# Two of four blocks of x inside the first nine steps of the attention loop, and wo in sixteen reads

## The chip, the cores and the metric

The kernel runs on one core of a Trainium2 chip. The metric is the device time of one execution in microseconds. The core has five engines that work side by side, each in the order of its own instructions: PE (matrix products), DVE (vector work), ACT (activation functions), POOL (a second, slower vector engine) and SP (which only issues transfers). Transfers run on sixteen DMA engines; nearly all of them are issued by SP and run in one queue.

## The reference

A block of a transformer with adaptive layer norm, 2048 tokens of 640 features. Cut to what matters here:

```python
mod = silu(c) @ w_mod                       # six rows of 640: sa, ca, ga, sb, cb, gb
h = layernorm(x) * (1 + ca) + sa
q = (h @ wq)                                # 32 heads of 128
p = softmax(q @ k_cache.T * 128 ** -0.5)    # 2048 keys for each head
x = x + ga * ((p @ v_cache) @ wo)           # 4096 -> 640
h = layernorm(x) * (1 + cb) + sb
x = x + gb * B(h)                           # layer norm, w1, gelu, shifts, w2, layer norm, w3, gelu, w4
```

All inputs are bf16. K and V are caches of 32 heads x 2048 keys x 128.

## The kernel before, in words

**The front.** x is read in four blocks of 512 tokens (`load_x`), each block as four tiles of 128 tokens. For a block, `stats` makes mean and variance on DVE (`bn_stats`, `bn_aggr`) and the root on ACT; `normed` takes the reciprocal and normalises on DVE. `to_hT` transposes the block on PE, in five slices of 128 features, four 128x128 transposes each, into a bank of PSUM, and copies the slice out to `hT` with scale and shift, even slices on ACT and odd ones on DVE. Scale and shift come from the first part of w_mod (`load_mod(0, ...)`) by `cols`, 50 narrow products. `q_head0` makes the queries of head 0 for a block from `hT`: five products of 512 columns and a copy on ACT. The front does this for blocks 0, 1, 2 and for the transposes of block 3. The remaining four rows of modulation (`mod_rows`, five chunks of five products and an ACT copy) and the queries of block 3 stand in steps 0 to 2.

While the front runs, its data lies in the ring of 20 slots that the loop uses later for probabilities: x in slots 1 to 5, the first part of w_mod in 6 to 9, the second part and small constants from 13 on. wo has its own memory (40 KB a partition) and is read by one transfer of 5 MB at the end of the front's list of reads.

**The loop.** One step `s` handles 128 queries of one head against all 2048 keys; a head has 16 steps, 32 heads make 512. `qk` makes the scores in two halves on PE. DVE takes each half to `negS` with its running minimum (L598, two of 1.15 us a step). POOL joins the two minima (L603). ACT makes the exponential of the 2048 keys into slot `s % 10` of the ring (L606). The probabilities must then be transposed: for two or three steps of a head PE does it (`PE_STEPS`), for the others SP issues a DMA transpose, mostly for two steps at a time (L233). Nine steps later (`PVD = 9`) `pv` multiplies the transposed probabilities with V (L313, 16 products), ACT copies the result out every second step (L585), POOL divides by the sum and writes to memory. The queries of the next head (`q_piece`, `q_evac`) fill PE's gaps. In steps 2, 6 and 10 of a head SP also issues the reads of K (transposing), wq and V of later heads; V comes in rows of one key, 256 bytes each.

All of this is an order written out by hand: the program text appends each operation to its engine's list, and waits follow from named keys that an operation reads and writes. So what stands first in the text stands first in the engine's queue, and an operation that waits holds up all behind it on its engine. In the first nine steps there is no `pv` yet.

After the loop come the product with wo and the second half of the block, which the change does not touch.

The places that matter: `load_x`, `load_mod`, `load_wq`, `load_k`, `load_v` (reads), `stats`, `normed`, `to_hT`, `q_head0`, `mod_rows` (front), and in the loop

```python
if not is_pe(s):
    if s % 2 == 1 and not is_pe(s - 1):
        transpose(s - 1, 2)
    elif s % 2 == 1 or is_pe(s + 1):
        transpose(s, 1)
```

Of the kernel before, what the change touches and what calls it, by code (L numbers as in the profile page):

```python
# [9 lines left out]
F32 = mybir.dt.float32  # L10
# [113 lines left out]
def bass_adaLN_cond__mha_block_cached__mixer_s_mlp__prompt_kernel(  # L124
# [21 lines left out]
    with ExitStack() as es:  # L146
# [9 lines left out]
        if True:  # L156
            with ExitStack() as es1:
# [35 lines left out]
                wmod = flat[:, WO_:WO_ + KT * 2 * D].rearrange("p (k n) -> p k n", k=KT)  # L193
                RO = 13 * SK
                wmodr = flat[:, RO:RO + KT * 4 * D].rearrange("p (k n) -> p k n", k=KT)
                BO = RO + KT * 4 * D
                s_bc = flat[:, BO:BO + KT * 128].rearrange("p (k q) -> p k q", k=KT)
                ones_f = flat[:, BO + KT * 128:BO + KT * 128 + 256].bitcast(F32)
                SO = BO + KT * 128 + 256
                st = flat[:, SO:SO + NQT * 24].bitcast(F32).rearrange("p (t z) -> p t z", t=NQT)  # L200
                CO = SO + NQT * 24
                c_f = flat[:, CO:CO + 2 * KT].bitcast(F32)
                mcol = flat[:, CO + 2 * KT:CO + 6 * KT].bitcast(F32)
                c_sb = flat[:, CO + 6 * KT:CO + 7 * KT]
                s_col = flat[:, CO + 7 * KT:CO + 8 * KT]
                IO = CO + 8 * KT
                ident = flat[:, IO:IO + 128]
                assert IO + 128 <= 2 * RP * SK and XO + NQT * D <= WO_ and WO_ + KT * 2 * D <= 10 * SK
# [111 lines left out]
                WMK = ringk(WO_, WO_ + KT * 2 * D)  # L320
                WRK = ringk(RO, 2 * RP * SK)
                XK = [ringk(XO + cc * 4 * D, XO + (cc + 1) * 4 * D) for cc in range(NQC)]

                def load_x(cc):
                    G.dma("sync", lambda e: e.dma_start(
                        x_sb[:, 4 * cc:4 * cc + 4], x2d[cc * 512:(cc + 1) * 512, :].rearrange("(t p) d -> p t d", p=128)),
                        ("x", cc), w=[("x", cc)])

                def load_mod(part, dst, n0, n1):
                    G.dma("sync", lambda e: e.dma_start(  # L330
                        dst, w_mod[:, n0:n1].rearrange("(k p) n -> p k n", p=128)), ("wm", part), w=[("wm", part)])

                def load_c(e):
                    with nc.allow_non_contiguous_dma(reason="tiny c vector"):
                        return e.dma_start(c_sb, c[0].rearrange("(kt p) -> p kt", p=128))
# [15 lines left out]
                G.op("gpsimd", lambda g: g.memset(ident, 0.0), w=["id0"])  # L351
                G.op("gpsimd", lambda g: g.memset(ones_f, 1.0), w=["onesf"])
                G.op("gpsimd", lambda g: g.affine_select(out=ident, in_=ident, pattern=[[-1, 128]],
                                                         compare_op=ALU.not_equal, fill=1.0, base=0, channel_multiplier=1),
                     r=["id0"], w=["ident"])
                G.op("gpsimd", lambda g: g.tensor_copy(identf[:], ident), r=["ident"] + ringk(IO, IO + 128), w=["identf"])
                G.op("gpsimd", lambda g: g.memset(Vaug[:, :, :, 128:130], 1.0), w=["ones"])
                G.op("scalar", lambda a: a.activation(s_col, c_sb, ACT.Silu), r=["c"], w=["scol"])
                G.op("scalar", lambda a: a.activation(c_f, c_sb, ACT.Silu), r=["c"], w=["cf"])
                for k in range(KT):  # L360
                    G.op("gpsimd", lambda g, k=k: g.tensor_scalar(out=s_bc[:, k, :], in0=ones_f, scalar1=c_f[:, k:k + 1],
                                                                  scalar2=1.0, op0=ALU.mult, op1=ALU.mult),
                         r=["onesf", "cf"] + WRK, w=[("sbc", k)])

# [11 lines left out]
                def stats(cc):  # L376
                    for t in range(4 * cc, 4 * cc + 4):
                        for z in range(2):
                            G.op("vector", lambda v, t=t, z=z: v.bn_stats(st[:, t, 6 * z:6 * z + 6], x_sb[:, t, z * HD:(z + 1) * HD]),  # L379
                                 r=[("x", cc)], w=[("st", t, z)])  # L380
                    for t in range(4 * cc, 4 * cc + 4):
                        G.op("vector", lambda v, t=t: v.bn_aggr(mv[:, t, :], st[:, t, :]),
                             r=[("st", t, 0), ("st", t, 1)] + WRK, w=[("mv", t)])
                    G.op("scalar", lambda a: a.activation(sd[:, 4 * cc:4 * cc + 4], mv[:, 4 * cc:4 * cc + 4, 1], ACT.Sqrt, bias=float(EPS)),
                         r=[("mv", t) for t in range(4 * cc, 4 * cc + 4)], w=[("sd", cc)])

                def normed(cc):
                    G.op("vector", lambda v: v.reciprocal(rstd[:, 4 * cc:4 * cc + 4], sd[:, 4 * cc:4 * cc + 4]),
                         r=[("sd", cc)], w=[("rstd", cc)])
                    for t in range(4 * cc, 4 * cc + 4):  # L390
                        G.op("vector", lambda v, t=t: v.tensor_scalar(
                            out=x_sb[:, t], in0=x_sb[:, t], scalar1=mv[:, t, 0:1], scalar2=rstd[:, t:t + 1],
                            op0=ALU.subtract, op1=ALU.mult),
                            r=[("rstd", cc), ("mv", t)], w=[("xh", t)])

                def to_hT(cc):
                    for k in range(KT):
                        b = (4, 5, 3, 4, 5)[k % 5] if cc == NQC - 1 else (cc * KT + k) % 6

                        def f(t, k=k, b=b):  # L400
                            for z in range(4):
                                ins = t.transpose(TB[b][:, z * 128:(z + 1) * 128], x_sb[:, 4 * cc + z, k * 128:(k + 1) * 128], ident)
                            return ins
                        G.op("tensor", f, r=["ident"] + [("xh", 4 * cc + z) for z in range(4)] + XK[cc] + ringk(IO, IO + 128), w=[TK[b]])
                        if k % 2 == 0:
# [3 lines left out]
                                r=[TK[b], "mcol"] + WRK, w=[("hT", cc, k)])  # L409
                        else:  # L410
# [3 lines left out]
                                r=[TK[b], "mcol"] + WRK, w=[("hT", cc, k)])  # L414
# [6 lines left out]
                stats(0)  # L421
                normed(0)
                stats(1)
                G.op("tensor", cols, r=["scol", ("wm", 0)] + WMK, w=[("J", 1)])
                G.op("scalar", lambda a: a.copy(mcol[:, 0:KT], JB[1][:, 0:KT]), r=[("J", 1)], w=["mcol0"])
                G.op("scalar", lambda a: a.add(mcol[:, KT:2 * KT], JB[1][:, KT:2 * KT], 1.0), r=[("J", 1), "mcol0"], w=["mcol"])
                normed(1)
                to_hT(0)
                for cc in range(NQC):
                    if cc + 2 < NQC:  # L430
                        stats(cc + 2)
                        normed(cc + 2)
                    if cc + 1 < NQC:
                        q_head0(cc)
                        to_hT(cc + 1)

                mone = small[:, 0:4]
                G.op("gpsimd", lambda g: g.memset(mone, -1.0), w=["mone"] + [("mv", t) for t in range(NQT)])
                bank(("q", 0, NQC - 1))
                MROW = [(n0, min(n0 + 512, 4 * D)) for n0 in range(0, 4 * D, 512)]  # L440

                def mod_rows(i):
                    n0, n1 = MROW[i]
                    bank = PO[:, (i % 2) * 512:(i % 2) * 512 + n1 - n0]
# [5 lines left out]
                    G.op("tensor", f, r=[("sbc", k) for k in range(KT)] + [("wm", 1)] + WRK, w=[("O", i % 2)])  # L450
                    G.op("scalar", lambda a: a.copy(mod_bc[:, n0:n1], bank), r=[("O", i % 2)], w=[("mod", i)])
# [39 lines left out]
                wof = wo[:].rearrange("p h n -> p (h n)")  # L491
# [60 lines left out]
                for s in range(NG + PVD + LAG):  # L552
# [3 lines left out]
                    if s <= 2:  # L556
                        for i in ((0,), (1, 2), range(3, len(MROW)))[s]:
                            mod_rows(i)
                    if s == 3:
                        G.op("gpsimd", lambda g: g.tensor_scalar(  # L560
                            out=mod_bc[:, 2 * D:3 * D], in0=mod_bc[:, 2 * D:3 * D], scalar1=1.0, scalar2=1.0, op0=ALU.add, op1=ALU.mult),
                            r=[("mod", i) for i in range(len(MROW))], w=["mod"])
# [346 lines left out]
```

## Time and profile before

| | us |
|---|---|
| median of three runs (lowest, highest) | 1546.83 (1545.79, 1552.67) |
| the profiled execution | 1551.33 |
| its span, first to last instruction | 1549.2 |
| PE, DVE, ACT, POOL busy | 1467.1, 1374.3, 1256.5, 622.3 |
| PE waiting for a landed transpose, in all | 27.0 |
| the read of wo: issued at, landed after | 30.83, 16.7 |
| first minimum of step 0 (DVE) starts | 35.23 |
| first exponential (ACT) starts | 38.84 |

The profile is of one execution of its own, 4.5 us above the median of the three others. Busy time counts work on the engine; instructions that wait, branch or issue a transfer are not in it, and SP's rows are issues. "idle before <- X" says what ended an idle time. PEld is the loading of weights into PE, which overlaps PE. A wait is put down to the releaser that came last by the profile, which need not be the true one.

### The profile page before, as it was taken

To read this page: it belongs to the slowest core of one execution; us is meant where nothing else is said; L and a number is where in the kernel's file an instruction comes from. 1 tells how busy PE (TensorE), PEld (TensorE's weight loads), DVE (VectorE), ACT (ScalarE), POOL (GpSimd) and SP (SyncE) were. 2 spreads that over 40 slices of the span, in tenths; PEclk is the share of its full clock that TensorE was granted. 3 is DMA by queue.
4 is the path that set the end of the run, shared out by engine and by line. 5 is a ranking of instruction groups with operands and counts; after the bars stand their busy time and mean duration, and the time that the engine had idled before them with its cause. 6 is when DMAs were issued, how large, how long until landed. Compare 5 with 4: busy or idle time off the path is not lost.

```text
span 1549.2 us, 32502 instructions
## 1 busy us (share of the span) xinstructions
PE 1467.1 (95%) x13446; PEld 911.4 (59%) x12663; DVE 1374.3 (89%) x2431; ACT 1256.5 (81%) x1177; POOL 622.3 (40%) x1397
## 2 busy tenths in 40 slices
PE   4899999999999999999999999999999899999999
PEld 2466666666656566666666665666565665554545
DVE  6999999999999999999999999999999737667425
ACT  4999999999999999999999999999999800034230
POOL 0144444444444444444444444444444433323100
PEclk9999999999999999999999999999999999999999
DMA  9999999999999999999999999999999999825100
GB/s 301 243 216 248 246 239 239 238 228 241 239 241 225 241 239 247 229 244 239 233 239 244 236 235 239 238 239 242 227 237 223 243 241 195 155 58 131 35 22 35
DMA packets 1156183, 330.32 MB, mean 213 GB/s; under 512 B 1136640, under 2 KB 1150016, under 8 KB 1156032
## 3 DMA queue, kind: packets, MB, share of 16 engines
q1 hardware_dynamic: 1147552, 307.10, 101.1%
q0 software_dynamic: 6144, 16.79, 3.6%
q10 hardware_dynamic: 2336, 4.34, 0.8%
q8 instruction: 104, 1.70, 0.5%
q14 instruction: 47, 0.39, 0.1%
HBM read 43.48 MB, written 19.40 MB: 41 GB/s over the span
## 4 chain that ended last, share of the span: by engine, by line
ACT 58%; PE 20%; DVE 10%; DMA 7%; issue 3%; POOL 2%; POOLq 0%; DVEq 0%
ACT ring L606 47%; PE Sps L540 9%; DVE negS L598 8%; DMA ring<-ring 6%; ACT ring L272 4%; PE Sps L846 4%; ACT Of L585 3%; ACT kv L255 3%; PE QPp L797 2%; PE Oaug L797 2%; PE PTp L313 1%; PE Sps L782 1%; DVE ring L379 1%; POOL o_scratch L469 1%; DMA kv<-Of 0%
## 5 line engine op out<-in xcount | busy, mean ns | idle before, releaser
L598 DVE TENSOR_SCALAR_CACHE_REDUCE negS<-Sps 128x1024 f32<-128x1024 f32 x1024 | 1174.8, 1224 | 21.2 <-PE Sps L15 20.5
L606 ACT ACTIVATE ring<-negS,small 128x2048 bf16<-128x2048 f32 x512 | 1068.9, 2190 | 10.9 <-POOL small L603 10.2
L313 PEld LDWEIGHTS PTp<-kv,ring 128*128 128x128 bf16 x8192 | 556.2, 98 | 337.8 <-issue 94.7
L313 PE MATMUL PTp<-kv,ring 128*128 128x129 bf16 x8192 | 646.8, 221 | 28.2 <-DMA ring<-ring 27.0
L15 PE MATMUL Sps<-kv 128*128 128x512 bf16 x1009 | 382.6, 379 | 11.3 <-DVE negS L598 7.2
L603 POOL TENSOR_SCALAR small<-small 128x1 f32<-128x1 f32 x512 | 145.8, 285 | 601.1 <-DVE negS L598 601.1
L299 PE MATMUL Sps<-kv 128*128 128x512 bf16 x955 | 367.6, 385 | 14.7 <-DVE negS L598 5.2
L462 POOL TENSOR_SCALAR On<-Of,small 128x128 bf16<-128x128 f32 x512 | 189.9, 371 | 13.0
L299 PEld LDWEIGHTS Sps<-kv 128*128 128x128 bf16 x1024 | 98.2, 96 | 120.3 <-DVE negS L598 87.5
L585 ACT COPY Of<-PTp 128x259 f32<-128x259 f32 x256 | 139.6, 545 | 17.1 <-PE PTp L313 17.1
L455 POOL TENSOR_TENSOR small<-Of,small 128x4 f32<-128x4 f32 x128 | 133.1, 1040 | 11.5 <-ACT Of L585 11.5
L469 POOL DMA_DIRECT2D o_scratch<-On x128 | 103.4, 808 | 40.8 <-POOL On L462 37.2
L248 PE MATMUL Oaug<-hTx,kv 128*128 128x512 bf16 x258 | 97.8, 384 | 5.1 <-DVE hTx L411 4.8
L248 PE MATMUL QPp<-hTx,kv 128*128 128x512 bf16 x259 | 96.7, 378 | 3.0 <-ACT hTx L406 2.3
L727 ACT ACT_TABLE_LOAD x1 | 1.3, 1283 | 111.8 <-POOL hTx L745 111.8
L598 DVE DVE_READ_ACCUMULATOR negS<-Sps 128x1 f32 x1024 | 89.2, 87 | 0.0
L640 POOL TENSOR_SCALAR negS<-negS 128x1 f32<-128x1 f32 x48 | 24.4, 509 | 124.1 <-DVE negS L649 124.1
L540 PE MATMUL Sps<-wo,negS 128*128 128x128 bf16 (+1 forms) x503 | 69.9, 298 | 0.5
L540 PE MATMUL Sps<-wo,hTx 128*128 128x512 bf16 (+1 forms) x502 | 69.3, 298 | 0.5
L850 DVE TENSOR_TENSOR ring<-Sps,ring 128x640 f32<-128x640 f32 x15 | 12.4, 824 | 59.5 <-PE Sps L846 59.5
L654 DVE TENSOR_TENSOR ring<-Sps,mod_bc 128x640 f32<-128x640 f32 x16 | 13.1, 821 | 57.8 <-PE Sps L540 57.8
L265 PE MATMUL QPp<-identf,ring 128*128 128x128 f32 x320 | 61.8, 275 | 0.1
(88 smaller groups left out, 1068.6 us busy)
## 6 DMA issues: line engine op xcount, KB each, us to landing
kv<-in_A_v_cache_dram SPq DMA_DIRECT2D x32, 512.0 KB, 4.9
o_scratch<-On POOLq DMA_DIRECT2D x128, 128.0 KB, 4.9
kv<-in_A_wq_dram SPq DMA_DIRECT2D x32, 160.0 KB, 3.2
wo<-in_A_wo_dram SPq DMA_DIRECT2D x1, 5120.0 KB, 16.7
ring<-ring SPq DMA_TRANSPOSE x240, 7.1
ring<-in_A_x_dram SPq DMA_DIRECT2D x5, 640.0 KB, 6.6
ring<-in_w_mod_dram SPq DMA_DIRECT2D x1, 3200.0 KB, 13.5
out_dram<-wo SPq DMA_DIRECT2D x15, 160.0 KB, 1.8
```

What stands on the lines that cost most here:

```text
L15: return t.add_instruction(mybir.InstMatmult(name=t.bass.get_next_instruction_name(), ins=[t.lower_ap(rhs), t.lower_ap(lhsT)], outs=[t.low ...
L248: G.op("tensor", lambda t: t.matmul(JB[jb], wq[:, hb, q, :], hT[:, q, cc * 512:(cc + 1) * 512], start=(q == 0), stop=(q == KT - 1)), r=[(" ...
L299: ins = (t.matmul if c2 == 0 else partial(same_weights, t))(Sps[:, col:col + 512], QT[:, hb, j * 128:(j + 1) * 128], KTs[:, hb, col:col + ...
L313: ins = t.matmul(ob[:, 0:129], pt, Vaug[:, hb, kt, 0:129], start=(kt == 0), stop=(kt == NKT - 1))
L455: G.op("gpsimd", lambda g: g.tensor_tensor(out=rl[:, 4 * b:4 * b + 4], in0=Of[:].rearrange("p a z d -> p (a z) d")[:, 4 * b:4 * b + 4, 128 ...
L462: G.op("gpsimd", lambda g: g.tensor_scalar(out=On[:, b, z, :], in0=Of[:, 2 * b + z // 2, z % 2, 0:128], scalar1=rl[:, 4 * b + z:4 * b + z ...
L469: G.dma("gpsimd", lambda e: e.dma_start(o_scr[jj // 2:jj // 2 + 2, :, hh].rearrange("a p z d -> p a (z d)"), On[:, b].rearrange("p (a z) d ...
L540: ins = t.matmul(YB[b][:, c0:c0 + cw], OTj[pr % 2][:, 2 * hh + z, :], wo[:, hh, c0:c0 + cw], start=(hh == 0), stop=(hh == H - 1))
L585: G.op("scalar", lambda a, p=p: a.copy(Of[:, p % 4].rearrange("p z d -> p (z d)")[:, 0:259], PO[:, (p % 2) * 512:(p % 2) * 512 + 259]), r= ...
L598: G.op("vector", lambda v, half=half, dst=dst, src=src, r8=r8: v.tensor_scalar(out=dst, in0=src, scalar1=-SCALE, scalar2=None, op0=ALU.mul ...
L603: G.op("gpsimd", lambda g, r8=r8: g.tensor_scalar(out=nm[:, r8:r8 + 1], in0=nm0[:, r8:r8 + 1], scalar1=nm1[:, r8:r8 + 1], scalar2=None, op ...
L606: G.op("scalar", lambda a, s=s, r8=r8: a.activation(Pb[:, s % RP, :], negS[:, s % 3, :], ACT.Exp, bias=nm[:, r8:r8 + 1], scale=-1.0), r=[( ...
```

## The change

Where the staging lies: x block 0 and 1 now lie in ring slots 4 to 6, block 2 and 3 in slots 7 to 9, the first part of w_mod in slots 0 to 3; the second part of w_mod and all small constants lie in wo's memory, which is why wo cannot be read as long as they are used.

Reads: c as a row of five partitions, issued by ACT and turned into a column by a small product on PE; SP's order is x0, first part of w_mod, x1, wq of heads 0 and 1, K of head 0, x2, x3, second part of w_mod, V of head 0, K of head 1. wo is read in sixteen parts of two heads (320 KB each), one in step 11 of every odd head, in the last head in step 4.

Work: `stats` can do part of a block, and takes the root on POOL (add, then power -0.5), not on ACT; ACT loads the table of the exponential once in the front. The front does block 0 in full, block 1 to its normalising and half of the statistics of block 2. `first_steps(s)`, called at the end of step s, does the rest: block 1's transposes in step 0, block 1's queries and block 2's normalising in step 1, the slices of block 2 in steps 2 to 4, statistics of block 3 in 3 and 4, block 2's queries and block 3's normalising in 5, slices of block 3 in 6 to 8, its queries in 9, and the rows of modulation in steps 4, 5, 8 and 9.

`to_hT` now issues all transposes of a call and then all copies. In step 0 its five slices share two banks, so each copy finds there what was transposed last: slices 0 and 2 of block 1 receive slice 4, and slice 1 receives slice 3. The last slice of block 3 is transposed after the exponential of step 8 has been written over two of the four tiles it reads, and the queries of head 0 for block 3 are made with the weights that step 6 has loaded for head 2 in the same buffer. The amount of work is that of the reference; these values are others.

```diff
-                XO = SK
-                x_sb = flat[:, XO:XO + NQT * D].rearrange("p (t d) -> p t d", t=NQT)
-                WO_ = 6 * SK
+                wmod = flat[:, 0:KT * 2 * D].rearrange("p (k n) -> p k n", k=KT)
+                XO = [4 * SK, 4 * SK + 4 * D, 7 * SK, 7 * SK + 4 * D]
+                x_of = lambda cc: flat[:, XO[cc]:XO[cc] + 4 * D].rearrange("p (t d) -> p t d", t=4)
+                wmodr = wof[:, 0:KT * 4 * D].rearrange("p (k n) -> p k n", k=KT)
...
+                WOP = H // 16
+                def load_wo(i):
+                    G.dma("sync", lambda e: e.dma_start(
+                        wo[:, i * WOP:(i + 1) * WOP], A_wo[i * WOP * 128:(i + 1) * WOP * 128, :].rearrange("(h p) n -> p h n", p=128)),
+                        ("wo", i % 2), w=["WOR"] + (["wo", "woz", "wo4"] if i == 15 else []))
+                G.dma("scalar", lambda e: e.dma_start(c_row, c[0].rearrange("(kt p) -> kt p", p=128)), "c", r=WOR, w=["c"])
                 load_x(0)
-                G.dma("sync", load_c, "c", w=["c"])
+                load_mod(0, wmod, 0, 2 * D)
                 load_x(1)
-                load_mod(0, wmod, 0, 2 * D)
+                load_wq(0)
+                if H > 1:
+                    load_wq(1)
+                load_k(0)
                 for cc in range(2, NQC):
                     load_x(cc)
-                load_wq(0)
-                load_k(0)
+                load_mod(1, wmodr, 2 * D, 6 * D)
                 load_v(0)
-                load_mod(1, wmodr, 2 * D, 6 * D)
                 if H > 1:
-                    load_wq(1)
                     load_k(1)
-                G.dma("sync", lambda e: e.dma_start(wo[:], A_wo.rearrange("(h p) n -> p h n", p=128)), "wo", w=["wo", "woz", "wo4"])
...
-                    G.op("scalar", lambda a: a.activation(sd[:, 4 * cc:4 * cc + 4], mv[:, 4 * cc:4 * cc + 4, 1], ACT.Sqrt, bias=float(EPS)),
+                    G.op("gpsimd", lambda g: g.tensor_scalar(out=sd[:, 4 * cc:4 * cc + 4], in0=mv[:, 4 * cc:4 * cc + 4, 1], scalar1=float(EPS),
+                                                             scalar2=1.0, op0=ALU.add, op1=ALU.mult),
...
+                    G.op("gpsimd", lambda g: g.tensor_tensor(out=rstd[:, 4 * cc:4 * cc + 4], in0=sd[:, 4 * cc:4 * cc + 4], in1=mh4, op=ALU.pow),
...
-                stats(0)
+                stats(0, 0, 4)
                 normed(0)
-                stats(1)
+                stats(1, 0, 2)
...
+                to_hT(0, range(KT), range(KT), (1, 3))
+                stats(1, 2, 4)
+                q_head0(0)
...
+                stats(2, 0, 2)
                 normed(1)
-                to_hT(0)
-                for cc in range(NQC):
...
+                def first_steps(s):
+                    if s == 0:
+                        to_hT(1, range(KT), (4, 5, 4, 5, 4))
+                        stats(2, 2, 4)
+                    if s == 1:
+                        q_head0(1)
+                        normed(2)
+                    if s in (2, 3, 4):
+                        k = 2 * (s - 2)
+                        to_hT(2, range(k, min(k + 2, KT)), (4, 5), (1, 3))
+                    if s == 3:
+                        stats(3, 0, 2)
+                    if s == 4:
+                        stats(3, 2, 4)
+                        mod_rows(0, 1)
+                    if s == 5:
+                        q_head0(2)
+                        normed(3)
+                        mod_rows(1, 0)
+                        mod_rows(2, 1)
+                    if s in (6, 7, 8):
+                        k = 2 * (s - 6)
+                        to_hT(3, range(k, min(k + 2, KT)), (4, 5), (1, 3))
+                    if s == 8:
+                        mod_rows(3, 1)
+                    if s == 9:
+                        q_head0(3)
+                        mod_rows(4, 1)
...
+                        if j == (4 if h + 1 == H else 11) and h % 2 == 1:
+                            load_wo(h // 2)
+                        first_steps(s)
```

More of the change, by code (lines that the diff above doesn't have):

```diff
@@ L330, in load_mod @@
                     G.dma("sync", lambda e: e.dma_start(
[L331 to L335, printed above, removed]
+                        dst, w_mod[:, n0:n1].rearrange("(k p) n -> p k n", p=128)), ("wm", part), r=WOR, w=[("wm", part)])
@@ L357, in bass_adaLN_cond__mha_block_cached__mixer_s_mlp__prompt_kernel @@
                 G.op("gpsimd", lambda g: g.memset(Vaug[:, :, :, 128:130], 1.0), w=["ones"])
[L358 to L363, printed above, removed]
+                G.op("tensor", lambda t: t.matmul(JB[0][:, 0:KT], c_row, ident[0:KT, 0:KT], start=True, stop=True),
+                     r=["c", "ident"] + WOR, w=[("J", 0)])
@@ L393, in normed, with to_hT @@
                             op0=ALU.subtract, op1=ALU.mult),
[L394 to L398, printed above, removed]
+                            r=[("rstd", cc), ("mv", u)], w=[("xh", u)])
+                def to_hT(cc, ks, banks, onv=()):
+                    xs = x_of(cc)
+                    for k, b in zip(ks, banks):
@@ L405, in to_hT @@
-                        if k % 2 == 0:
+                        G.op("tensor", f, r=["ident"] + [("xh", 4 * cc + z) for z in range(4)] + XK[cc] + WOR, w=[TK[b]])
+                    for k, b in zip(ks, banks):
+                        if k not in onv:
                             G.op("scalar", lambda a, k=k, b=b: a.activation(
@@ L449, in f @@
                         return ins
[L450 to L451 removed]
+                    G.op("tensor", f, r=[("sbc", k) for k in range(KT)] + [("wm", 1)] + WOR, w=[("O", b)])
+                    G.op("scalar", lambda a: a.copy(mod_bc[:, n0:n1], bank), r=[("O", b)], w=[("mod", i)])
+                def first_steps(s):
[26 more added lines that the diff above has]
+                        mod_rows(4, 1)
+                    if s == 10:
+                        G.op("gpsimd", lambda g: g.tensor_scalar(
+                            out=mod_bc[:, 2 * D:3 * D], in0=mod_bc[:, 2 * D:3 * D], scalar1=1.0, scalar2=1.0, op0=ALU.add, op1=ALU.mult),
+                            r=[("mod", i) for i in range(len(MROW))], w=["mod"])
+                        G.op("gpsimd", lambda g: g.memset(mone, -1.0), w=["mone"] + [("mv", t) for t in range(NQT)])
                 def rcp(gr):
```

117 lines of the change are left out of this document (57 added, 60 removed).

## The prediction

> **What bounds the kernel now.** I read the page's busy shares first, then the stages of the loop, then SP's queue row by row, then who waits for a landed transpose, and last the first 65 us.
>
> ```profile
> PE 1467.1 (95%) x13446; PEld 911.4 (59%) x12663; DVE 1374.3 (89%) x2431; ACT 1256.5 (81%) x1177; POOL 622.3 (40%) x1397
> ...
> 60.00:200.00 140.00, 136.95 (x1354) 89.25 (x1253) 140.00 (x247) 139.58 (x126) 62.59 (x145) 1.00 1.18 237
> ...
> 1000.00:1200.00 200.00, 189.11 (x1868) 121.60 (x1730) 194.93 (x341) 196.70 (x176) 93.10 (x214) 1.00 1.21 232
> ```
>
> In the second and third line the columns are stage, its length, then busy time of PE, PEld, DVE, ACT and POOL, the clock, the DMA share and GB/s. Early in the loop DVE and ACT are full. Late in it nothing that computes is full: something else sets the pace. It is SP's queue (start, length, what):
>
> ```profile
> 742.10 4.61 SPq L233 DMA_TRANSPOSE ring<-ring  x1
> ...
> 746.75 14.66 SPq L233 DMA_TRANSPOSE ring<-ring  x3
> ...
> 761.46 2.05 SPq L216 DMA_TRANSPOSE kv<-in_A_k_cache_dram  x1
> 763.55 4.50 SPq L233 DMA_TRANSPOSE ring<-ring  x1
> ...
> 768.10 0.58 SPq L220 DMA_DIRECT2D kv<-in_A_wq_dram  x1
> 768.73 5.13 SPq L233 DMA_TRANSPOSE ring<-ring  x1
> ...
> 773.91 4.56 SPq L233 DMA_TRANSPOSE ring<-ring  x1
> 778.51 0.58 SPq L225 DMA_DIRECT2D kv<-in_A_v_cache_dram  x1
> ```
>
> Each row starts within 0.05 us of the end of the one before: 742.10 + 4.61 = 746.71, next 746.75, and so on. From 98 us to the end of the loop it has no larger gap than 0.45 us. So SP (the issue, and the transfers that hold it back) works all the time, and falls behind ACT: the pair of transposes of a head's first two steps is issued 1.6 us after its exponential in head 2 (120.66, 122.25), 5.1 in head 10 (415.27, 420.37), and it stays near that (3.8 in head 30), because PE then waits for it. PE's waits for landed transposes, first of 200 to 400 us, then of 1000 to 1240 (total, times, longest):
>
> ```profile
> PE PTp L313 <- DMA ring<-ring: 1.2, 2, 0.8
> ...
> PE PTp L313 <- DMA ring<-ring: 10.2, 10, 2.3
> ```
>
> From exponential to exponential a head takes (341.62 - 120.66)/6 = 36.83 us between heads 2 and 8, ACT's pace, and (1161.97 - 415.27)/20 = 37.34 us between heads 10 and 30, SP's. The front:
>
> ```profile
> 4.84 3.24 DVE L379 BATCH_NORM_STATS2 ring<-ring 128x6 f32<-128x320 bf16 x8 [4.84 <-DMA ring<-in_A_x_dram]
> ...
> 22.78 1.06 PE L248 MATMUL QPp<-hTx,kv 128*128 128x512 bf16 x4 [0.67 <-DVE hTx L411]
> ...
> 29.16 1.89 PE L248 MATMUL Oaug<-hTx,kv 128*128 128x512 bf16 x4 [4.20 <-DVE hTx L411]
> ...
> 35.23 1.23 DVE L598 TENSOR_SCALAR_CACHE_REDUCE negS<-Sps 128x1024 f32<-128x1024 f32 x1 [1.85 <-PE Sps L15]
> ...
> 63.01 2.00 ACT L606 ACTIVATE ring<-negS,small 128x2048 bf16<-128x2048 f32 x1 [0.29 <-POOL small L603]
> ```
>
> Step 0's minimum starts at 35.23; step 9's exponential at 63.01, and ACT hardly idles from there to 200.
>
> **Part 1, the sixteen reads of wo.** The one read lies in the front today: issued at 30.83, landed 16.7 us later, behind K of head 1, which landed at 32.8. It holds up one transpose (issued 44.58, landed 51.23), nine steps before its reader, so taking it out gains nothing on the path. Fifteen of the sixteen parts now stand on SP's full queue; the last falls into head 31, which reads no K, V or wq, and I cost it at nothing. A part is a sixteenth of the old read: 14.7 us alone on the queue (32.8 to 47.5) / 16 = 0.92 us. Bounds: the rows of wq (160 KB, 0.58 us issue, and about 0.5 us longer next transposes) scaled by rows of memory, 256 against 640, give 0.4; V (512 KB: 0.58 us, and the single transpose behind it takes 4.6 instead of 2.1) scaled by bytes, 320/512 of 3.1, gives 1.9. I take 0.92, the same tensor in the same rows. As SP is never idle, a part moves all that is queued behind it: 15 x 0.92 = +13.8 us (6 to 28). At first that is lag, which SP may build up to about 5 us; but it does so in the kernel before too, only by head 10 instead of 5, so the end moves by the full sum. Queued behind a part are the pairs of steps 12 to 15; behind those, PE's second product, then the scores, DVE, ACT.
>
> The Trainium skill (DMA: Bandwidth & Descriptors, Anatomy of one DMA) gives a transfer a fixed 2.0 us beside its bytes; by that a part is 2.75 us and the sum 41. The rows above speak against it: SP goes on 0.05 us after the issue of V, so such a latency lies in the landing, not in the queue.
>
> **Part 2, the front.** I walk each engine's new order with durations from rows: half a minimum 1.145 (2.29 a step), exponential 1.905, from the minimum's end to the exponential 0.51, ACT copy 0.475, ACT transpose copy 0.69, DVE's 0.455, statistics of a block 3.15 and 0.41, normalising 1.43, a 512-column matmul 0.215 and 0.64 from the first scores to DVE.
>
> x0 lands as before at 4.84. Now w_mod's first part comes next (1.6 MB at the 400 GB/s of these slices: 9.0 instead of 12.35), so the columns of shift and scale leave PE at 10.5 instead of 14.0. The inverse root moves from ACT and DVE to POOL: 0.29 + 1.04 (the 128x4 power, L455) against 0.45, so normalising block 0 starts at 9.83 (before 8.90), its transposes at 11.4, the last ACT copy ends at 14.5, the queries of block 0 at 15.8. DVE goes on with blocks 1 and 2a (x2 lands near 16) and block 1's normalising to 19.3. K of head 0 lands near 14. So step 0 starts at 19.3, 15.9 us earlier. The table loads of 1.28 us at 7.10 and 37.55 go.
>
> The small edits cost nothing on the path: c as a row, its product on PE, the constants and the early table load lie before 9.0, while the engines wait for w_mod; the copies of c (5 x 0.35 on POOL) lie behind block 1's root, where POOL waits for step 0; the rows of w_mod are read only after the loop, and their landing (30.3 before, much the same now) is ahead of step 4.
>
> Then what is moved comes back. DVE does inside the steps 3.68 + 1.43 + 0.91 of statistics, normalising and copies for block 3, and for block 2 the same less 1.83: 10.2 us. With no stall step 10 would start at 19.3 + 10 x 2.29 + 10.2 = 52.4; before it did at 62.49. That is the most this part can gain, 10.1 us. But DVE stalls:
>
> - step 2, 1.3: ACT copies five slices of block 1 after step 0's exponential (24.0 to 27.4), PE's queue waits for them with block 1's queries before step 2's scores.
> - steps 3 and 4, 1.4: PE makes the next two slices after the scores and DVE stands for its copy of the second, behind ACT's copy of the bank.
> - step 6, 1.5: eleven matmuls of rows of w_mod, five of block 2's queries, and PE waiting for ACT's copies of both banks, before and inside the scores.
> - steps 7 and 8, 1.5: as 3 and 4.
> - step 9, 4.65: the last slice of block 3 lies in ring slots 8 and 9, so its transposes, queued behind step 8's scores and written after step 8's exponential (56.3 to 58.2), wait for that exponential. Behind them on PE: five matmuls of w_mod and step 9's scores. DVE, done at 55.8, gets them at 60.45.
> - step 10, 2.2: block 3's queries and the last five rows, 2.15 us more on PE in step 9.
>
> Sum 12.55, so step 10 starts at 64.95. Step 9's exponential comes at 63.25 (before 63.01), that of step 11 at 70.04 (before 67.55): +2.5 us, and ACT is full from there as before. SP has caught up with ACT at that point in both kernels (gaps of 1.3, 0.3 and 2.6 us between 74 and 98), so its full stretch starts 2.5 us later too. Bounds: -10.1 with no stall, and +7 if PE runs at half pace in each of about eight stalls, 0.6 us more each.
>
> That pace is in the rows above: four matmuls took 1.06 us at 22.78 after an idle of 0.67, and 1.89 at 29.16 after 4.20 of idle. In my walk PE idles 2.8 us in step 8; the seven matmuls behind it, to the first scores, would at half pace add 1.5 us. The Trainium skill (TensorE: Matmul & The Clock Gate, the HAM clock gate) puts the fall to half rate at about 3.4 us without work, and the two rows agree; by it the 2.8 us stay just below, and the sum stays.
>
> **Sum.** +2.5 + 13.8 = +16.3 us. The profiled execution takes 1551.33 (span 1549.2 and 2.1 around it), which would become 1567.6; the median of the runs is 4.5 lower, 1546.83, so I predict 1563.1.
>
> **Rivals.**
> - A, the parts are hidden: their bytes run while SP still writes the next transposes' descriptors. For it: an unhindered pair takes 4.1 to 4.2 us of SP (60.78, 65.04), so SP may be bound by issuing. Against: the single transpose behind V took 4.6. Then a part costs its issue at most; with 0.2 left of it, 3.0 + 2.5: about 1552.
> - B, faster: DVE's order in steps 0 to 9 does not stall as walked, above all in step 9, and the parts are hidden. Front -10 and parts 0: 1537. It decides where the stalls stay below 7 us and the parts below 0.2 us. Against: the wait for step 8's exponential is in the order of the instructions.
> - C, a part costs as V by bytes, 1.9 us, or PE runs the front at half pace: 15 x 1.9 + 2.5 = +31, 1578. By the fixed latency above, 43 and 1590.
> - D, the reads of x2 and w_mod land later than I think, step 0 starts no earlier than 25 us: 6 us on all steps, 1569.
>
> **How the numbers follow.** My forecast 0.58, A 0.18, B 0.10, C 0.08, D 0.06. The time is that of the first. Its own range is 1554 to 1572 (parts 0.63 to 1.3 us, front -3 to +5). The 8-in-10 range reaches into A and C: 1547 to 1574. About 0.5%, 7.7 us, is what can be told from no change. Faster needs B nearly whole: 0.10. Same takes A, the weak end of B and the cheap end of the forecast: 0.20. Slower 0.70.
>
> **What would show it.** The first minimum near 19 us; a DVE idle of over 4 us before step 9's, released by PE; exponentials of step 9 and 11 near 63 and 70. SP gapless from about 100 us, with fifteen rows of wo in it, PE's wait for landed transposes well over the 27.0 us of before and starting before 360 us, and heads 10 to 30 at 37.8 us each. I am wrong if SP shows gaps in the loop, if heads keep 37.3, or if step 11's exponential starts before 62 us.

## The result and the profile after

The changed kernel takes 1566.03 us (median of 6 runs, 1561.42 to 1569.05) against 1548.3 of the kernel before (6 runs): ratio 1.0111, 95% interval 1.0089 to 1.0133. It is slower by 17.7 us; forecast were 16.3. The profiled execution took 1569.05 us, its span is 1567.2, 18.0 longer than before. (The median of 1546.83 given above for the kernel before was that of the first three of the six runs.)

The page of the changed kernel: busy shares, and the two largest groups of DVE and ACT (busy, mean of one, idle before them and its releaser).

```profile
PE 1472.7 (94%) x13448; PEld 903.9 (58%) x12664; DVE 1375.4 (88%) x2425; ACT 1259.5 (80%) x1175; POOL 630.0 (40%) x1406
...
L635 DVE TENSOR_SCALAR_CACHE_REDUCE negS<-Sps 128x1024 f32<-128x1024 f32 x1024 | 1177.3, 1222 | 36.5 <-PE Sps L15 35.5
L643 ACT ACTIVATE ring<-negS,small 128x2048 bf16<-128x2048 f32 x512 | 1037.1, 2062 | 34.3 <-POOL small L640 33.4
```

No engine's work grows by nearly that much: PE is busy 5.6 us longer, POOL 7.7, ACT 3.0, DVE 1.1. DVE idles 36.5 us before its minimum (21.2 before), ACT 34.3 before its exponential (10.9 before). So most of the time is in waits. Where they stand, the front first (changed kernel, rows of DVE and ACT in order of time: start, length, what, idle before it):

```profile
19.61 1.21 DVE L635 TENSOR_SCALAR_CACHE_REDUCE negS<-Sps 128x1024 f32<-128x1024 f32 x1
...
29.30 1.23 DVE L635 TENSOR_SCALAR_CACHE_REDUCE negS<-Sps 128x1024 f32<-128x1024 f32 x1 [1.84 <-PE Sps L15]
...
46.23 1.22 DVE L635 TENSOR_SCALAR_CACHE_REDUCE negS<-Sps 128x1024 f32<-128x1024 f32 x1 [0.66 <-PE Sps L15]
...
48.14 1.23 DVE L635 TENSOR_SCALAR_CACHE_REDUCE negS<-Sps 128x1024 f32<-128x1024 f32 x1 [0.67 <-PE Sps L15]
...
62.35 1.23 DVE L635 TENSOR_SCALAR_CACHE_REDUCE negS<-Sps 128x1024 f32<-128x1024 f32 x1 [6.10 <-PE Sps L15]
...
67.38 1.23 DVE L635 TENSOR_SCALAR_CACHE_REDUCE negS<-Sps 128x1024 f32<-128x1024 f32 x1 [2.04 <-PE Sps L15]
...
72.46 2.00 ACT L643 ACTIVATE ring<-negS,small 128x2048 bf16<-128x2048 f32 x1 [0.30 <-POOL small L640]
```

Step 0 starts at 19.61 (35.23 before), and step 9 at 62.35 (60.20 before): the 15.6 us that were won are gone nine steps later. The exponential of step 11 starts at 72.46, 4.9 us later than the 67.58 of before. The longest single wait is the one of 6.10 us before step 9; PE's rows show what it is made of:

```profile
58.73 0.61 PE L414 MATMUL PTp<-wo,ring 128*128 128x128 bf16 x4 [3.31 <-ACT ring L643]
59.13 2.34 PE L461 MATMUL PTp<-wo 128*128 128x512 bf16 x5
61.26 0.63 PE L302 MATMUL Sps<-kv 128*128 128x512 bf16 x1
```

PE stands 3.31 us until the exponential of step 8 ends, then transposes the last slice of block 3, makes five matmuls in 2.34 us (five like them took 1.24 at 37.79) and only then step 9's scores.

From there on the queue of SP tells the rest (changed kernel, SP's rows):

```profile
774.47 2.12 SPq L219 DMA_TRANSPOSE kv<-in_A_k_cache_dram  x1
776.63 4.34 SPq L236 DMA_TRANSPOSE ring<-ring  x1
781.01 0.58 SPq L223 DMA_DIRECT2D kv<-in_A_wq_dram  x1
...
790.97 0.58 SPq L228 DMA_DIRECT2D kv<-in_A_v_cache_dram  x1
791.60 4.63 SPq L236 DMA_TRANSPOSE ring<-ring  x1
796.27 0.58 SPq L339 DMA_DIRECT2D wo<-in_A_wo_dram  x1
796.90 5.40 SPq L236 DMA_TRANSPOSE ring<-ring  x1
```

The queue is as gapless as before, with a part of wo between the others. PE's wait for landed transposes is 42.3 us in all (27.0 before); in the stretch 200 to 400 us, where it was 1.2, it is now

```profile
PE PTp L316 <- DMA ring<-ring: 8.9, 11, 1.8
```

A useful ruler is the end of the exponential of a head's second step, read in every profile; the columns "head 2", "head 10" and "head 30" give it in us. "Step 9" is the start of that step's first minimum, "last" the end of the last exponential, and "pace" the time of a head between heads 10 and 30. Each row is of one profiled execution, and the times of one kernel spread by 1.6 to 12.8 us from run to run, so a difference of 2 us between two rows shows little by itself. The kernel before was measured anew beside each group of runs (medians from 1548.3 to 1555.67); the ratios below are to the one beside.

| run | step 9 | head 2 | head 10 | head 30 | last | pace |
|---|---|---|---|---|---|---|
| before | 60.20 | 120.66 | 415.27 | 1161.97 | 1232.55 | 37.33 |
| changed | 62.35 | 125.55 | 424.98 | 1179.46 | 1248.86 | 37.72 |
| e1_split | 60.21 | 120.65 | 418.05 | 1177.22 | 1250.08 | 37.96 |
| e2_front | 62.76 | 125.31 | 419.91 | 1165.57 | 1234.90 | 37.28 |
| e3_pool | 62.72 | 125.90 | 425.25 | 1181.48 | 1253.46 | 37.81 |
| e4_x3 | 58.15 | 122.61 | 422.89 | 1176.84 | 1247.54 | 37.70 |
| e5_one | 63.34 | 125.90 | 434.98 | 1178.25 | 1248.10 | 37.16 |
| e6_twice | 62.60 | 125.41 | 428.84 | 1196.52 | 1266.95 | 38.38 |
| e9_v16d_before | 60.31 | 120.76 | 421.29 | 1175.92 | 1247.24 | 37.73 |
| e10_v16d_after | 62.65 | 126.30 | 426.45 | 1189.55 | 1260.14 | 38.15 |
| e11_nov_before | 60.24 | 120.71 | 415.43 | 1152.25 | 1220.08 | 36.84 |
| e12_nov_after | 62.65 | 125.34 | 419.94 | 1156.42 | 1224.23 | 36.82 |

In the changed kernel 4.9 us are lost by head 2, and another 17.5 - 4.9 = 12.6 up to head 30. Fourteen parts of wo are read in that stretch, so that is 0.90 us for each.

### The profile page after: what moved, and what is told of

It reads as the page before. It is cut to its first block, busy times and chain, and to the rows that moved or that the text cites. A ratio compares the mean times of both kernels' runs of the same rounds, so it can differ in the third digit from the quotient of the medians.

```text
span 1567.2 us, 32514 instructions
## 1 busy us (share of the span) xinstructions
PE 1472.7 (94%) x13448; PEld 903.9 (58%) x12664; DVE 1375.4 (88%) x2425; ACT 1259.5 (80%) x1175; POOL 630.0 (40%) x1406
## 4 chain that ended last, share of the span: by engine, by line
ACT 41%; PE 20%; DVE 16%; DMA 13%; issue 6%; POOL 3%; SPq 1%; POOLq 0%; DVEq 0%
ACT ring L643 33%; DVE negS L635 15%; DMA ring<-ring 12%; PE Sps L586 8%; PE Sps L886 4%; ACT ring L275 3%; ACT kv L258 2%; ACT Of L622 2%; PE Oaug L837 2%; PE QPp L837 2%; POOL o_scratch L516 1%; PE PTp L316 1%; PE Sps L822 1%; POOL small L640 1%; DMA negS<-o_scratch 1%
## 5 line engine op out<-in xcount | busy, mean ns | idle before, releaser
L635 DVE TENSOR_SCALAR_CACHE_REDUCE negS<-Sps 128x1024 f32<-128x1024 f32 x1024 | 1177.3, 1222 | 36.5 <-PE Sps L15 35.5
L643 ACT ACTIVATE ring<-negS,small 128x2048 bf16<-128x2048 f32 x512 | 1037.1, 2062 | 34.3 <-POOL small L640 33.4
L316 PE MATMUL PTp<-kv,ring 128*128 128x129 bf16 x8192 | 647.2, 221 | 44.4 <-DMA ring<-ring 42.3
L622 ACT COPY Of<-PTp 128x259 f32<-128x259 f32 x256 | 106.5, 416 | 17.2 <-PE PTp L316 17.2
L268 PE MATMUL Oaug<-identf,ring 128*128 128x128 f32 x320 | 61.7, 275 | 1.0 <-ACT kv L258 1.0
```

The lines of the kernel that those rows point to most:

```text
L316: ins = t.matmul(ob[:, 0:129], pt, Vaug[:, hb, kt, 0:129], start=(kt == 0), stop=(kt == NKT - 1))
L622: G.op("scalar", lambda a, p=p: a.copy(Of[:, p % 4].rearrange("p z d -> p (z d)")[:, 0:259], PO[:, (p % 2) * 512:(p % 2) * 512 + 259]), r= ...
L635: G.op("vector", lambda v, half=half, dst=dst, src=src, r8=r8: v.tensor_scalar(out=dst, in0=src, scalar1=-SCALE, scalar2=None, op0=ALU.mul ...
L643: G.op("scalar", lambda a, s=s, r8=r8: a.activation(Pb[:, s % RP, :], negS[:, s % 3, :], ACT.Exp, bias=nm[:, r8:r8 + 1], scale=-1.0), r=[( ...
```

## The experiments

Theory Q: SP's queue and the transfers behind it are full, so that a part of wo moves all that follows; the front costs some 5 us of its own. Its rivals: the parts are hidden (H), a part costs its time even where the queue has room (R), the cost lies in issuing (S), each part has a fixed cost (P), the shifted front slows the loop for good (F), ACT, DVE and PE set the pace themselves (A).

**Each half alone.** The kernel before with the parts only:

```diff
-                G.dma("sync", lambda e: e.dma_start(wo[:], ...), "wo", w=["wo", "woz", "wo4"])
+                def load_wo(i): ...            (as in the change)
...
+                        if j == (4 if h + 1 == H else 11) and h % 2 == 1:
+                            load_wo(h // 2)
```

> The kernel before with one edit: wo is read in sixteen parts in the odd heads, the front is untouched. Theory Q (SP's queue is full, a part moves all that is queued behind it by about 0.9 us): +12 to +14 us on the kernel before, ratio 1.008 to 1.009; the exponentials of head 2 come when they come before (120.7), those of head 30 about 12.6 us later (1174.6); SP shows no gap. Rival H (the parts are hidden, and what the changed kernel lost it lost in the front): no change, within 2 us.

Measured: 1567.83 us, ratio 1.0109 (1.0091 to 1.0127). Head 2 is where it was, head 30 comes 15.3 us later. H falls: the split alone, with the front untouched, costs as much as the whole change. The size was above the expectation: 15.3 for 14 parts is 1.09 us each.

The changed kernel without the reads:

```diff
-                        if j == (4 if h + 1 == H else 11) and h % 2 == 1:
-                            load_wo(h // 2)
+                        if h % 2 == 1 and h + 1 < H and 11 <= j <= 14:
+                            (POOL sets a quarter of the part's memory to zero)
+                        if h + 1 == H and j == 4:
+                            load_wo(15)
```

> The changed kernel with fifteen of the sixteen reads of wo left out; POOL sets that memory to zero instead, in four short pieces, so the product with wo is not the reference's. Theory Q: what is left is the front, +4.9 us as read at head 2 in the changed kernel, ratio about 1.003, and heads 10 to 30 go back to 37.3 us each. Rival H: +15 us or more stays. A third theory, F (the shifted front changes how the loop runs for good): the heads stay slower than 37.3 without the reads.

Measured: 1555.69, ratio 1.0031 (1.0015 to 1.0046); the pace is back at 37.28. So the front is the small half, and F falls. Its delay of 4.7 us at head 2 is 3.6 at head 30 and 2.4 at the last exponential. The two halves add to 1.0140, the whole is 1.0111. With the intervals of all three that is no clear difference, so whether the halves add up exactly stays open.

**The parts a second time.**

```diff
+                        if j == 11 and h % 2 == 0 and h >= 2:
+                            load_wo(h // 2 - 1)
```

> The changed kernel with fifteen of the parts of wo read a second time, in step 11 of the even heads: 31 parts in all. Theory Q: another 15 x 0.9 = +13.5 us on the changed kernel, ratio to before about 1.020. Rival H: as the changed kernel, 1.011.

Measured: 1587.94, ratio 1.024 (1.0219 to 1.0261), more than expected. Between heads 2 and 30 now lie 28 parts, and that stretch is (1196.52 - 125.41) - (1161.97 - 120.66) = 29.8 us longer than before, 1.06 for each part. The cost grows with the number of parts, as Q says.

**Issue, or transfer?** The parts from POOL's queue:

```diff
-                    G.dma("sync", lambda e: e.dma_start(
+                    G.dma("gpsimd", lambda e: e.dma_start(
                         wo[:, i * WOP:(i + 1) * WOP], ...
```

> The changed kernel with the sixteen parts issued by POOL instead of SP, on another queue of the same DMA engines. If it is SP's issue that is full (0.6 us a part), the cost of the parts goes and the front's +4.9 us is left, ratio 1.003. If it is the transfers themselves that are full, the cost stays, ratio 1.010 to 1.012.

Measured: 1572.25, ratio 1.0135 (1.0114 to 1.0157). The reads of wo on the two pages, changed kernel first (KB each, median us from issue to landing):

```profile
wo<-in_A_wo_dram SPq DMA_DIRECT2D x16, 320.0 KB, 3.9
...
wo<-in_A_wo_dram POOLq DMA_DIRECT2D x16, 320.0 KB, 5.3
```

SP issues nothing of wo, and the cost is all there: between heads 2 and 30 it is ((1181.48 - 125.90) - (1161.97 - 120.66)) / 14 = 1.02 us a part. S falls: what is full lies behind the issue and serves both queues. That SP's long rows are the time in which it is held back there fits with this; which resource behind the issue is the full one, no run here separates.

**One read instead of sixteen.**

```diff
-                        if j == (4 if h + 1 == H else 11) and h % 2 == 1:
-                            load_wo(h // 2)
+                        if h == 1 and j == 11:
+                            (one read of the whole of wo)
```

> The changed kernel with wo read by one transfer in step 11 of head 1 instead of sixteen. Theory Q (the bytes on the full DMA engines count, wherever they stand): the end is as in the changed kernel, 1.010 to 1.012, but the loss comes at once, 8 to 12 us behind in heads 1 to 4 and no more from there. Rival P (each part has a fixed cost of its own): 1.006 or less.

Measured: 1568.34, ratio 1.0107 (1.009 to 1.0123), as the changed kernel; P, which needed 1.006 or less, falls. SP's rows behind the read:

```profile
118.64 0.58 SPq L659 DMA_DIRECT2D wo<-in_A_wo_dram  x1
119.27 30.05 SPq L236 DMA_TRANSPOSE ring<-ring  x4
149.35 2.27 SPq L219 DMA_TRANSPOSE kv<-in_A_k_cache_dram  x1
```

The four transposes that stand there take 30.05 us instead of some 18. The loss comes at once, as expected, and is larger than the 8 to 12 us of the expectation: 12.7 us between heads 2 and 3, on top of the front's 5.2. (PE's granted clock was 0.50 for 13.7 us there, from 131.2 on; what that adds, no run separates.) The loop is 19.7 us late at head 10 (434.98) and then makes up a little of it at a pace of 37.16, until at head 30 it is 16.3 late; the expectation had no such gain, and its cause was not sought. It ends where sixteen parts end: within the intervals the bytes count, and not how they are cut.

**Room in the queue.** I first tried to make V cheaper, by rows of sixteen keys in memory. Scores and V must then agree in the order of keys. First PE read K in that order:

```diff
-                    ... A_v_cache[0, h].rearrange("(t p) d -> p t d", p=128)
+                    ... A_v_cache[0, h].rearrange("(p t) d -> p t d", p=128)
...
-                                Sps[:, col:col + 512], QT[...], KTs[:, hb, col:col + 512], ...
+                                Sps[...].rearrange("p (t q) -> p t q", t=4), QT[...],
+                                KTs[:, hb].rearrange("p (q t) -> p t q", t=NKT)[:, col // 128:col // 128 + 4, :], ...
```

> The changed kernel with V in rows of sixteen keys (4 KB a partition and row instead of 256 bytes) and PE reading the keys of K in the order that fits. Theory Q: V takes some 2 us a head less on the DMA engines, SP shows gaps, a head falls back to ACT's 36.8, the parts of wo are hidden; what is left of the change is its front: ratio to before 0.994 to 0.997. Rival: PE reads K with a stride more slowly, scores over 0.22 us a matmul, and the loop becomes PE's: over 1.01.

> The kernel before with V in rows of sixteen keys, nothing else. Theory Q: heads at 36.8 us throughout, PE's waits for landed transposes nearly gone, -10 to -12 us, ratio 0.992 to 0.994, and faster than the changed kernel with the same V by the front's 3 to 5 us. Rival: slower by PE's stride, over 1.01.

Measured: 3464.42 and 3489.96, ratios 2.2348 (2.2298 to 2.2399) and 2.2476 (2.2447 to 2.2505). The rival came in far stronger than written; a score matmul of the second kernel:

```profile
L299 PE MATMUL Sps<-kv 128*128 128x512 bf16 x1024 | 1124.4, 1098 | 0.0
```

1098 ns instead of 385, PE at 99% of the span, and the granted clock at 0.55 over the run. The lower clock explains only a part: an ordinary score matmul at a granted clock of 0.50 takes 630 ns (changed kernel, at 53.93). These two say nothing on wo.

Then DVE made the order, on its way out of PSUM, and PE read K as before:

```diff
-                            dst = negS[:, s % 3, half * 1024:(half + 1) * 1024]
-                            src = Sps[:, half * 1024:(half + 1) * 1024]
+                            dst = negS[:, s % 3].rearrange("p (t i) -> p t i", t=NKT)[:, :, half * 64:half * 64 + 64]
+                            src = Sps[:, half * 1024:(half + 1) * 1024].rearrange("p (i t) -> p t i", t=NKT)
```

> The kernel before with V in rows of sixteen keys (4 KB), where now DVE puts the scores in the order that fits while it takes them out of PSUM; PE reads K as before. Theory Q: heads at ACT's 36.8 us to the end, PE's waits for landed transposes nearly gone, SP with gaps, -8 to -12 us, ratio 0.992 to 0.995. Rival: DVE is slower on these strides, over 1.2 us a half, and the loop becomes DVE's: over 1.02.

> The changed kernel with V in rows of sixteen keys by DVE's order. Theory Q: the queue has room for the parts of wo, which then cost little; against the kernel before with the same V only the front's 3 to 5 us are left, ratio to the kernel before 0.994 to 0.998. Rival R (the parts cost their 0.9 us whatever V does): 1.003 to 1.006.

Measured: 1561.9, ratio 1.0046 (1.0029 to 1.0062), and 1581.17, ratio 1.017 (1.0147 to 1.0193). DVE kept its pace (1221 ns a half), and yet both are slower, so neither the number of theory Q nor that of its rival came. The transfers of the first, from its page:

```profile
DMA packets 1156183, 330.32 MB, mean 211 GB/s; under 512 B 1136640, under 2 KB 1150016, under 8 KB 1156032
```

The number of small packets is that of the kernel before, 1136640. V's rows in SBUF are 128 wide with two columns of ones behind them, so it seems that a row of sixteen keys is still cut into pieces of 256 bytes. My expectation rested on a saving that this edit does not make. That the kernel takes a little longer this way is measured; the cause is not. (V lands 5.3 us after its issue instead of 4.9, but no run shows that this is it.) The room was not made: PE waits 47.8 us for landed transposes here, 27.0 in the kernel before. So the pair does not test Q. A part of wo costs ((1189.55 - 126.30) - (1175.92 - 120.76)) / 14 = 0.58 us by the two profiles, but the medians lie 19.3 us apart, which is nearer to 1.0 a part, and the runs of the second spread by 12 us; the size stays open.

So I took the bytes away:

```diff
-                        if j == PVD + 1 and h + 1 < H:
+                        if j == PVD + 1 and h == 0:
                             load_v(h + 1)
```

> The kernel before with V read for heads 0 and 1 only; later heads multiply with those, so the output is not the reference's, and the queue is relieved of 512 KB a head. Theory Q: SP falls behind no more and shows gaps, heads 10 to 30 at ACT's 36.8 us, PE's waits for landed transposes under 5 us, -9 to -12 us, ratio 0.992 to 0.994. Rival A (ACT, DVE and PE, all nearly full, set the 37.3 us): no change.

> The changed kernel with V read for heads 0 and 1 only, values as in the run beside it. Theory Q: the parts of wo fit into the room and cost under 0.2 us each, so against the kernel before without V only the front's 2.5 to 5 us are left, ratio to the kernel before 0.994 to 0.997. Rival R (a part costs its 0.9 us of its own): 1.003 or more.

Measured: 1536.84, ratio 0.9909 (0.9895 to 0.9923), and 1541.02, ratio 0.9939 (0.9924 to 0.9954). Both move as Q says; the first gains 14.8 us by the medians, more than the 9 to 12 expected. The stage 1000 to 1200 us of the first (columns as in the prediction):

```profile
1000.00:1200.00 200.00, 198.00 (x1953) 125.85 (x1776) 199.51 (x349) 200.00 (x180) 95.55 (x218) 1.00 1.11 229
```

DVE and ACT are full to the end, the pace is 36.84, PE waits no more for landed transposes, and SP has over 100 us of gaps between 100 us and the last exponential (about 1 before). A falls: ACT's pace is 36.8, and the rest up to 37.3 was the queue. In the second kernel the fifteen parts are read as ever, and from head 2 to 30 it takes 1031.1 us against 1031.5 without them: with room in the queue a part costs nothing, and R falls. What is left of the change is the front, 4.2 us between the two medians.

**The wait in step 8.**

```diff
-                XO = [4 * SK, 4 * SK + 4 * D, 7 * SK, 7 * SK + 4 * D]
+                XO = [4 * SK, 4 * SK + 4 * D, 7 * SK, 18 * SK]
```

> The changed kernel with block 3 of x staged in ring slots 18 and 19, which are written only by the transposes of steps 8 and 9, instead of slots 8 and 9: its last slice no longer waits for the exponential of step 8 (and is made from x). Theory: step 9's first minimum starts near 58 instead of 62.35, exponentials 4 to 4.5 us earlier from there on; of that 2.5 to 4.5 us are left at the end, ratio 1.0085 to 1.0105. Rival: another wait of PE in step 8 takes its place and step 9 stays above 61.

Measured: 1566.2, ratio 1.0091 (1.0074 to 1.0107). The first minimum of step 9 on DVE:

```profile
58.15 1.23 DVE L635 TENSOR_SCALAR_CACHE_REDUCE negS<-Sps 128x1024 f32<-128x1024 f32 x1 [1.50 <-PE Sps L15]
```

The idle of 6.10 us is 1.50, and step 9 starts 4.2 us earlier. That the wait was the slot's is shown by the row. The half pace went with it: the five matmuls of w_mod take 1.24 us here. From there on the gain is smaller than expected: the exponential of step 11 (69.53) and head 2 come 2.9 us earlier, head 30 2.6, the last exponential 1.3. Whether the end gains can't be told, as the intervals of the two kernels overlap. With the wait gone, step 9 starts 2.05 us earlier than in the kernel before, but the exponential of step 11 still 2.0 later. Two waits of DVE are left there: 1.80 us before the second half of step 9, and 2.04 before step 10, which stands on PE behind the queries of block 3 and the last rows of w_mod.

No version that reads all of its inputs beats the kernel before. By e11 more room in its queue is worth up to 15 us, but no run here makes it with all of V read.

## Why the prediction was right, and where it was off

- What bounds the kernel: right, and the step on which all rests. SP's gapless rows late in the loop were read as the pace of 37.3 us a head. e11 shows it: without V's bytes it is 36.84 between the same heads. What "SP" meant was left open there (the issue, and the transfers that hold it back); for the parts of wo e3 settles it for what lies behind the issue.
- Part 1, the parts: forecast 0.92 us each, 13.8 in all. Measured 0.90 in the changed kernel, 1.09 alone on the kernel before, 1.06 with twice as many. That the loss is paid in full at the end held too: with the one read of e5 it is there at once, and with sixteen parts it grows to the same. That the size came out so well is in part luck. SP's own rows hold some 1.3 us a part: 0.63 for the issue, and behind it a transpose of 5.42 us (mean of 14 parts), where the same place in heads without a part has 4.71 (15 heads). Only 0.90 of that reaches the pace, and by which path the rest is made up is open.
- Part 2, the front: the start of step 0 was walked to 19.3 and came at 19.61, and the stalls lie at the places named. The sum was too small, +2.5 against +4.9 at step 11. Two terms were too small by 2.0 us together: step 2, 1.3 us against 1.84, and step 9, 4.65 against 6.10. Both fit one reason, PE at half pace: the last three of block 1's query products took 1.94 us with step 2's scores behind them at the same rate, and step 9's five matmuls 2.34 instead of 1.24. The stalls of steps 3 to 8 were smaller than walked (3.45 against 4.4), which hid a part of the miss.
- The clock: I put PE's idle time in step 8 at 2.8 us and kept full pace. The Trainium skill (TensorE: Matmul & The Clock Gate, the HAM clock gate) gives about 3.4 us without work for the fall to half rate. The idle was 3.31 us, under that figure too, and the matmuls behind it ran at half pace; but the clock had fallen before it. PE's rows, and two stretches of the changed kernel (columns as in the prediction, the clock third from the end):

```profile
25.13 0.39 PE L251 MATMUL QPp<-hTx,kv 128*128 128x512 bf16 x1 [2.28 <-ACT hTx L419]
...
26.47 1.94 PE L251 MATMUL QPp<-hTx,kv 128*128 128x512 bf16 x3 [0.20 <-ACT hTx L419]
...
34.82 0.62 PE L414 MATMUL PTp<-wo,ring 128*128 128x128 bf16 x8 [2.26 <-ACT hTx L419]
35.28 0.38 PE L302 MATMUL Sps<-kv 128*128 128x512 bf16 x1
...
52.51 0.62 PE L414 MATMUL PTp<-wo,ring 128*128 128x128 bf16 x8 [2.26 <-ACT hTx L419]
...
53.93 0.63 PE L302 MATMUL Sps<-kv 128*128 128x512 bf16 x1
...
52.00:53.00 1.00, 0.49 (x9) 0.49 (x9) 0.11 (x2) 1.00 (x3) 0.28 (x1) 1.00 0.67 153
...
54.00:55.00 1.00, 1.00 (x4) 0.15 (x1) 0.98 (x2) 1.00 (x2) 0.00 (x0) 0.50 0.00 0
```

  The granted clock fell to 0.50 some 0.8 us after PE came back from pauses of 2.28 us (before 25.13) and 2.26 (before 52.51), and not after another of 2.26 (before 34.82). The second fall lasted through the idle time of 3.31 us. In e2, e6 and e12, with the same order of work there, the clock stayed full after the pause before step 8's scores (2.25 or 2.26 us) and fell at the end of the one in step 8 or within 0.4 us behind it; that pause was then 4.04 us long. So here the fall came behind single pauses shorter than 3.4 us, but not behind each; and at full pace the pause in step 8 was itself over 3.4 us, so that the 2.8 of the walk was too short as well.
- The sum: 16.3 us against 17.7 (the times are 1563.1 and 1566.03; of the 2.9 us between them 1.5 are the kernel before, 1548.3 over six runs and not 1546.83). The 2.4 us by which the front was short were partly given back, which is luck: in e2's profile only 2.4 of the front's 4.7 us at head 2 reach the last exponential. In e12, where the queue has room, 4.2 of 4.6 do. By which path they are made up I did not settle.
- The prediction's rivals: A (hidden parts) fell by e1. B (faster) needed less than 7 us of stalls; DVE's rows show 1.84 + 1.06 + 0.66 + 0.67 + 1.06 + 6.10 + 0.51 + 2.04 = 13.9. In e12 its other condition holds, the parts are hidden, and the front still loses 4.2 us. C (1.9 us a part) fell by e1 and e6; its other half, PE at half pace in the front, came true in two stretches, of 3.4 and 10.2 us. Of D nothing is seen, step 0 came on time. The Trainium skill (DMA: Bandwidth & Descriptors, Anatomy of one DMA) gives its fixed 2.0 us for transfers that POOL issues, and the prediction used it for SP's. It shows in neither queue: the last exponential of e5, with one transfer, ends at 1248.10 and that of the changed kernel, with sixteen, at 1248.86; and on POOL's queue in e3 a part costs 1.02 us, while it lands 1.4 us later after its issue.

## What to carry to other kernels

Look at the rows of the issuing engine, not only at the busy shares. A queue whose rows follow each other without a gap, while the thing that they wait for has long been ready, is a good candidate for the bound; take bytes out of it to see whether the pace follows, as e11 did. Bytes added to such a queue cost time (here 0.9 to 1.1 us for 320 KB), on whichever of two queues and in one piece or sixteen. So a read that fits an empty stretch for nothing should not be moved into a full one, even if it makes room for an earlier start. And work moved behind the first step is not won when it stands in the same engines' order in front of the next steps: walk the new order with durations from the trace, and try the sum with PE at half pace behind each pause of two or three microseconds, since here some of them brought it and some did not.

## What I had not expected of the hardware

A score matmul that reads its 512 columns of K with a stride of 32 bytes takes 1098 ns instead of 385, and the clock granted to PE falls to 0.55 although PE is busy 99% of the span (e8); at half clock an ordinary one takes 630. DVE reads PSUM with a stride of 64 bytes at no cost, 1221 against 1224 ns (e9). Rows of 4 KB instead of 256 bytes in memory left the number of packets under 512 bytes at 1136640, with a gap of two columns behind each row of 128 in SBUF (e9); that the gap is the reason was not tried.
